# Seven half-depth products for eight in the gates and values of four chunks

## The chip, the core and the metric

The kernel runs on one core of a Trainium2 chip. It is one program, launched once; the metric is device microseconds of that core. Its engines are TensorE (PE in the profile, with PEld for its weight loads), VectorE (DVE), ScalarE (ACT) and GpSimd (POOL); SyncE (SP) issues most DMAs. Each engine takes its own instructions in the order of the program and waits at semaphores for the others.

## The reference

An attention with a learned position bias feeds a gated layer. What matters here is the second half:

```python
attn_out = _attn_ref(q, k, v, w1, b1, w2)                    # (4, 8, 576, 64)
x = attn_out.transpose(0, 2, 1, 3).reshape(2304, 512)
gate = 1.0 / (1.0 + np.exp(-(x @ w_gate)))                   # w_gate (512, 1536)
val = x @ w_val                                              # w_val  (512, 1536)
out = (gate * val) @ w_out                                   # w_out (1536, 512)
```

The weights come in as 64-bit floats, seen as pairs of 32-bit words; the kernel narrows them to 32 bits itself.

## The kernel before

The program has three stages: the position bias, the attention (32 units of one batch and two heads) and the gated layer, class `Moe`. The layer starts near 360 us, when the last unit of the attention leaves.

**Tiling.** The 2304 tokens are six chunks of `T = 384`; the 1536 hidden features are 12 blocks f of 128. For one pair of chunk c and block f, `gates` (L864) makes two products over a depth of 512 into the PSUM banks pg (gate) and pu (value). Every operand is split into a high part, which the matmul takes as it is, and a low part, the rest; a product is then high x high, high x low and low x high. So one product of 128 features by 384 tokens is 4 pieces of the depth x 3 = 12 matmuls of 384 columns, and a pair (c, f) has 24. `gated` (L875) forms g = sigmoid(pg) * pu on ACT and DVE and splits it into gh and gl. `outs` (L886) multiplies it by block f of w_out: 3 tiles of 128 tokens, 3 matmuls of 512 columns each, 9 in all, added up over f in the banks po. pg and pu have one bank each, po three banks for each of two chunks.

**Order.** The order on each engine is the order of the recording code (`run`, L904). The first 24 pairs follow the list ORDER (L46): chunk 0 (A) and chunk 1 (B) take turns, A leading, while the weights are made. After each pair `convert` (L848) moves the pipeline of weight blocks on: `stage` loads a raw block (512 KB), `narrow` makes 32-bit numbers of it with one ACT and four DVE instructions (L188 to L200), `upper` (L835) copies the high part on ACT and `lower` (L841) subtracts it on DVE. 30 of the 36 blocks (f and three kinds: gate z = 0, value z = 1, w_out z = 2) are made in this stretch; six were narrowed earlier and wait in DRAM (`scratch`). All split weights then stay in SBUF, in the pools wa, wb and wfirst.

The remaining 48 pairs are chunks 2 to 5, block by block. The next chunk's x is prepared meanwhile (`x_steps`, L946; for chunk 2 by XAFTER from the pair B5 on, the arithmetic from B9 on): two halves of the head sums are added, multiplied by the reciprocal softmax sum, and split.

What stands around the change on the queues: SP issues the loads of raw blocks, of x (xin) and reciprocals (xrec), and the stores, in the order of recording; POOL has no arithmetic in the layer after the attention's last pieces, since the sum of the head halves runs on DVE for all chunks but the first (XENG, L59).

## Time and profile before

| | us |
|---|---|
| median of 3 runs (lowest to highest) | 821.5 (821.01 to 823.13) |
| profiled execution | 824.66 |
| its span, first to last instruction | 822.5 |
| PE busy in the span | 794.6 (97%) |
| DVE busy | 506.2 (62%) |
| ACT busy | 431.0 (52%) |
| POOL busy | 260.8 (32%) |

The profile is of one execution. The span is what its rows cover; 2.2 us of the execution lie outside it. A matmul's row runs on while the next one streams, so rows overlap: the pace of PE is read from the starts of successive matmuls, or from the chain of waits, whose pieces do not overlap. A DVE row too can begin a little before the one ahead has ended.

### The profile page before, as it was taken

Reading aid. Unit: us, or ns where it says so; the run is one execution under the profiler, and the core shown is the slowest. Engines: PE = TensorE matmul, PEld = TensorE weight load, DVE = VectorE, ACT = ScalarE, POOL = GpSimd, SP = SyncE. Lnnn points to the kernel's source line nnn. Section 1 sums busy time; section 2 is a strip of 40 time slices with the busy share of each in tenths; the row PEclk is TensorE's granted clock in tenths of the full one; section 3 lists DMA queues with packets and bytes.
Section 4 is the critical chain, followed back from the end, with each engine's and each line's share of the span. In section 5 each row is a group of like instructions: output and inputs, shape, how many; then the busy total and the mean of one; then the engine's idle time right before and its main releaser. Section 6 shows DMA issues by size and latency. Waiting matters only on the chain.

```text
span 822.5 us, 16931 instructions
## 1 busy us (share of the span) xinstructions
PE 794.6 (97%) x6500; PEld 744.9 (91%) x6500; DVE 506.2 (62%) x1097; ACT 431.0 (52%) x914; POOL 260.8 (32%) x312
## 2 busy tenths in 40 slices
PE   7999989999999999879999999999999999999998
PEld 4888879999999998868999989999999999999997
DVE  6788789999899899977888784223311321241111
ACT  6888679898898998754444442211221221122112
POOL 1333569998999979730000000000000000000000
PEclk9999999999999999999999999999999999999999
DMA  5533236556466486569632302301030112011001
GB/s 193 170 104 116 67 87 169 148 149 181 142 171 178 122 229 189 175 188 314 228 94 63 100 2 77 97 21 29 10 116 1 40 48 68 4 35 39 1 1 38
DMA packets 51134, 86.40 MB, mean 105 GB/s; under 512 B 5616, under 2 KB 27248, under 8 KB 51056
## 3 DMA queue, kind: packets, MB, share of 16 engines
q1 hardware_dynamic: 48752, 81.87, 33.8%
q10 hardware_dynamic: 2304, 3.47, 1.3%
q8 instruction: 51, 0.84, 0.4%
q14 instruction: 27, 0.22, 0.1%
HBM read 60.08 MB, written 15.80 MB: 92 GB/s over the span
## 4 chain that ended last, share of the span: by engine, by line
PE 80%; DVE 10%; ACT 5%; issue 2%; DMA 2%; POOL 0%; POOLq 0%; SPq 0%; DVEq 0%; ACTq 0%
PE pu L872 18%; PE pg L872 17%; PE po L893 17%; PE sc L550 8%; PE acc L635 7%; PE pt L573 6%; PE bps L343 3%; PE y L319 2%; ACT ind L324 2%; DVE btmp L351 2%; DVE en L554 1%; PE pt L593 1%; DVE bias L359 1%; ACT en L557 1%; DVE aL L473 1%
## 5 line engine op out<-in xcount | busy, mean ns | idle before, releaser
L881 DVE TENSOR_TENSOR g<-pu,g 128x384 f32<-128x384 f32 x72 | 40.1, 557 | 204.3 <-PE pu L872 197.2
L872 PE MATMUL pg<-xhi,w 128*128 128x384 f32 x576 | 160.4, 339 | 3.7 <-ACT g L880 2.7
L872 PE MATMUL pu<-xhi,w 128*128 128x384 f32 x576 | 159.2, 336 | 0.4 <-DVE w L844 0.4
L893 PE MATMUL po<-w,gh 128*128 128x512 f32 x432 | 133.8, 391 | 0.0
L557 ACT ACTIVATE en<-en,mn 128x576 f32<-128x576 f32 x144 | 111.6, 775 | 31.4 <-DVE mn L554 30.4
L882 ACT ACTIVATE gh<-g 128x384 fp32r<-128x384 f32 x72 | 37.8, 525 | 145.3 <-DVE g L881 145.3
L550 PE MATMUL sc<-k,QS 128*128 128x288 f32 x640 | 111.5, 300 | 1.3 <-DVE bias L359 0.6
L872 PEld LDWEIGHTS pg<-xhi,w 128*128 128x128 f32 x576 | 105.6, 189 | 7.7 <-ACT g L880 3.1
L872 PEld LDWEIGHTS pu<-xhi,w 128*128 128x128 f32 x576 | 105.2, 188 | 1.0 <-DVE w L844 1.0
L554 DVE CUSTOM_DVE_ANT_0 en<-sc,bias 128x576 f32<-128x576 f32 x128 | 93.9, 752 | 7.4 <-PE sc L550 6.4
L872 PE MATMUL pg<-xlo,w 128*128 128x384 f32 x288 | 97.3, 338 | 0.2 <-DVE xlo L807 0.2
L872 PE MATMUL pu<-xlo,w 128*128 128x384 f32 x288 | 96.8, 336 | 0.0
L550 PEld LDWEIGHTS sc<-k,QS 128*128 128x128 f32 x640 | 91.7, 188 | 2.4 <-PE sc L550 0.8
L893 PEld LDWEIGHTS po<-w,gh 128*128 128x128 f32 x432 | 80.1, 188 | 12.0
L880 ACT ACTIVATE g<-pg 128x384 f32<-128x384 f32 x72 | 35.0, 487 | 106.1 <-PE pg L872 106.1
L573 PE MATMUL pt<-ident,en 128*128 128x128 f32 x576 | 87.1, 274 | 3.7 <-DVE aL L473 1.9
L893 PE MATMUL po<-w,gl 128*128 128x512 f32 x216 | 84.2, 390 | 0.0
L635 PE MATMUL acc<-aH,vv 128*128 128x288 f32 x240 | 75.7, 332 | 3.4 <-DVE xe L638 3.2
L573 PEld LDWEIGHTS pt<-ident,en 128*128 128x128 f32 x576 | 68.5, 141 | 7.2 <-ACT en L557 3.4
L473 DVE TENSOR_TENSOR aL<-pt,aH 128x512 fp32r<-128x512 f32 (+1 forms) x112 | 66.7, 607 | 7.2 <-ACT aH L472 7.2
L343 PE MATMUL bps<-cfs,ind 128*128 128x64 bf16 x1458 | 67.4, 193 | 3.0 <-DVE bias L359 2.2
L324 ACT ACTIVATE ind<-y 128x576 bf16<-128x576 f32 x100 | 62.4, 658 | 11.1 <-PE y L319 8.9
(121 smaller groups left out, 1425.9 us busy)
## 6 DMA issues: line engine op xcount, KB each, us to landing
kr<-in_k_dram SPq DMA_DIRECT2D x32, 288.0 KB
QS<-part SPq DMA_DIRECT2D x64, 144.0 KB, 2.7
xs<-xe SPq DMA_DIRECT2D x32, 288.0 KB, 3.4
xin<-xs SPq DMA_DIRECT2D x48, 192.0 KB, 3.4
vr<-in_v_dram SPq DMA_DIRECT2D x16, 320.0 KB, 3.4
qr<-in_q_dram SPq DMA_DIRECT2D x16, 288.0 KB
xrec<-rs SPq DMA_DIRECT2D x48, 96.0 KB, 3.6
ww<-in_moe_w_val_dram SPq DMA_DIRECT2D x9, 512.0 KB, 7.1
```

Source lines behind the costliest of these rows:

```text
L324: nc.scalar.activation(out=o, in_=y[:, :, 0:HF], func=AF.Sigmoid, scale=float(2.0 ** 64))
L343: nc.tensor.matmul(out=o, lhsT=st, rhs=cfs[:, part], start=(part == 0), stop=(part == 2))
L473: return lambda: nc.vector.tensor_tensor(out=lo, in0=ps, in1=hi.bitcast(F32), op=ALU.subtract)
L550: nc.tensor.matmul(out=ps[:, e, 0:HF], lhsT=l, rhs=r[:, HF * e:HF * e + HF], start=(i == 0), stop=(i == len(mms) - 1))
L554: nc.vector.tensor_tensor_reduce(out=half(en), in0=ps[:, :, 0:HF], in1=half(nbias), scale=-0.125, scalar=3.0e38, op0=ALU.add, op1=ALU.min, ...
L557: nc.scalar.activation(out=en, in_=en, func=AF.Exp, bias=mn, scale=-1.0, accum_out=sm)
L573: nc.tensor.transpose(pt[:, J], en[:, 128 * J:128 * J + 128], ident)
L635: nc.tensor.matmul(out=acc[:, 0:HF], lhsT=l, rhs=r, start=(i == 0), stop=(i == len(mms) - 1))
L872: self.nc.tensor.matmul(out=(pg, pu)[z], lhsT=l, rhs=r, start=(kc == 0 and i == 0), stop=(kc == 3 and i == 2))
L881: nc.vector.tensor_tensor(out=g, in0=pu, in1=g, op=ALU.mult)
L882: nc.scalar.activation(out=gh, in_=g, func=AF.Copy)
L893: self.nc.tensor.matmul(out=po, lhsT=l[:, tt], rhs=r, start=(f == 0 and i == 0), stop=(f == self.NF - 1 and i == 2))
```

## The change

Chunks 0 and 1 are computed as before. Chunks 2 and 3 (q = 1), then 4 and 5 (q = 2), are taken as a pair, blocks f = 2k and 2k + 1 as a pair, and the depth of 512 as two halves of 256. Gate (z = 0) and value (z = 1) of such a group are then a 2 x 2 by 2 x 2 product of blocks, made by the scheme with seven products and fifteen sums in place of eight products. One `half` (q, k, z) is seven products of 2 x 3 = 6 matmuls of 384 columns; there are 24 halves.

- Sums of x (`x_sums`): the four blocks B11 to B22 of a chunk pair and T1 to T4. POOL adds the head halves and makes the differences, DVE scales, ACT and DVE split the seven that are used. For q = 1 this is recorded between the pairs A and B, nine items after each from the 15th on; for q = 2 one item after each product, from the third half on.
- Sums of weights (`w_sums`): for each half the narrowed blocks are read again from DRAM, POOL makes four sums of 128 x 256, ACT and DVE split four tiles. This runs one to three halves ahead.
- So every narrowed gate and value block is now also written to `scratch`, and every split w_out block to `parts` (`keep`), from where it is read again for each chunk pair (`load_wo`).
- Sums of the products (`evict`): ACT copies the first product out of its bank, DVE does seven additions of a bank and an SBUF tile for each half. The banks pg and pu take turns, so product j + 2 needs the bank of product j.
- The output products of one group (12 tiles of 3 matmuls) stand one behind each product of the next group's first twelve products.
- SBUF pools: split weights share 13 slots of wa, raw blocks 15 of wb, which are given up for the x sums in the 15th pair; gates and their temporaries share 18 tiles.

```diff
+PRODUCTS = (("A11", "B11"), ("A12", "B21"), ("S2", "T2"), ("S3", "T3"), ("S1", "T1"), ("A22", "T4"), ("S4", "B22"))
@@ begin
+        def keep():
+            if z == 2:
+                nc.sync.dma_start(out=self.parts[f], in_=self.wts[b][2].bitcast(F32))
+            elif b not in self.pre:
+                nc.sync.dma_start(out=self.scratch[b], in_=m)
-        self.going[n] = steps + [(3, upper), (4, lower)]
+        self.going[n] = steps + [(3, upper), (4, lower), (6 if z == 2 else 4, keep)]
@@ x_sums
+            def add(n, t=t):
+                nc.gpsimd.tensor_tensor(out=t[n], in0=i[:, 0], in1=i[:, 1], op=ALU.add)
+            def scale(n, t=t):
+                nc.vector.tensor_tensor(out=t[n], in0=t[n], in1=t.pop((n, "rec")), op=ALU.mult)
+            def less(n, a, b, t=t):
+                nc.gpsimd.tensor_tensor(out=t[n], in0=t[a], in1=t[b], op=ALU.subtract)
+            def high(n, t=t, kc=kc):
+                nc.scalar.activation(out=var[n][:, 0, kc], in_=t[n], func=AF.Copy)
+            def low(n, t=t, kc=kc):
+                nc.vector.tensor_tensor(out=var[n][:, 1, kc], in0=t[n], in1=var[n][:, 0, kc].bitcast(F32), op=ALU.subtract)
+            for w in ("lB11 lB12 +B11 *B11 lB22 +B12 hB11 *B12 lB21 +B22 -B11 T1=B12-B11 *B22 +B21 hT1 T2=B22-T1 *B21 -T1 "
+                      "T3=B22-B12 hT2 hB22 T4=B21-T2 -T2 -B22 hT3 hB21 -T3 -B21 hT4 -T4").split():
@@ w_sums
+            for o, a, b, op in ((t[1][:, 0:2], m[:, 1, 0:2], m[:, 1, 2:4], ALU.add), (t[1][:, 2:4], t[1][:, 0:2], m[:, 0, 0:2], ALU.subtract),
+                                (t[2][:, 0:2], m[:, 0, 0:2], m[:, 1, 0:2], ALU.subtract), (t[2][:, 2:4], m[:, 0, 2:4], t[1][:, 2:4], ALU.subtract)):
+                nc.gpsimd.tensor_tensor(out=o, in0=a, in1=b, op=op)
@@ half
+            for kc in range(2):
+                for l, r in ((0, 0), (0, 1), (1, 0)):
+                    nc.tensor.matmul(out=p, lhsT=W[i][:, l, at + kc], rhs=V[b][:, r, kc], start=(n == 0), stop=(n == 5))
+        def add(o, p, x):
+            nc.vector.tensor_tensor(out=o, in0=p, in1=x, op=ALU.add)
+        for j in range(7):
+            p = product(j)
+            late, self.late = self.late, []
+            if self.now:
+                s = self.now.pop(0)()
...
+            evict(j, p)
+            for f in late:
+                f()
...
+            if nxt:
+                if j < 4:
+                    nxt[2][j]()
+                if 1 <= j < 5:
+                    nxt[3][j - 1]()
...
+            if self.fill:
+                self.fill.pop(0)()
@@ run
-        order += [(c, f) for c in range(2, NC) for f in range(NF)]
+            for h in range(len(self.halves)):
+                if h % NF == 2 and h < NF:
+                    self.fill = self.x_sums(2)
+                self.half(h)
```

On DVE, before, between the g of the pair A8 and the g of the next pair, B7 (g is the gated product, w a weight block, wm and ww its narrowed and raw form):

```order
881 L881 TENSOR_TENSOR g<-pu,g 128x384
882 L883 TENSOR_TENSOR gl<-g,gh 128x384
883 L844 TENSOR_TENSOR w_9_8317<-wm,w_9_8317 128x512
884 L194 TENSOR_SCALAR wm<-wm 128x512
885 L197 SCALAR_TENSOR_TENSOR wm<-ww,wm 128x512
886 L200 SCALAR_TENSOR_TENSOR wm<-ww,wm 128x512
887 L191 TENSOR_SCALAR wm<-wm 128x512
888 L881 TENSOR_TENSOR g<-pu,g 128x384
```

One weight block's worth of work stands between the two. The same place in the changed kernel (xt is a block of x or a difference T, xq its split form; L890 is the g):

```order
882 L890 TENSOR_TENSOR g<-pu,g 128x384
883 L892 TENSOR_TENSOR gl<-g,gh 128x384
884 L847 TENSOR_TENSOR w_9_8362<-wm,w_9_8362 128x512
885 L197 TENSOR_SCALAR wm<-wm 128x512
886 L200 SCALAR_TENSOR_TENSOR wm<-ww,wm 128x512
887 L203 SCALAR_TENSOR_TENSOR wm<-ww,wm 128x512
888 L194 TENSOR_SCALAR wm<-wm 128x512
889 L955 TENSOR_TENSOR xq<-xt,xq 128x384
890 L941 TENSOR_TENSOR xt<-xt,xrec 128x384 x2
891 L955 TENSOR_TENSOR xq<-xt,xq 128x384
892 L890 TENSOR_TENSOR g<-pu,g 128x384
```

Four instructions of the x sums now stand ahead of the second g; over the six pairs from B6 to A10 it is 19 of them, all ahead of the last value block of the weights.

On POOL, before, the end of its program:

```order
285 L466 TENSOR_SCALAR vv_7223<-vr 128x5x64
286 L477 TENSOR_TENSOR vv_7223<-vr,vv_7223 128x5x64
287 L761 MEMSET sig 128x1
288 L978 UNCONDITIONAL_BRANCH
289 L978 ISA
```

After the attention's last split POOL has nothing left. In the changed kernel the sums of x and then of the weights (ws, from a reloaded pair of blocks wm) follow there:

```order
287 L765 MEMSET sig 128x1
288 L938 TENSOR_TENSOR xt<-xin 128x384 x3
289 L945 TENSOR_TENSOR xt<-xt 128x384
290 L938 TENSOR_TENSOR xt<-xin 128x384
291 L945 TENSOR_TENSOR xt<-xt 128x384 x3
292 L938 TENSOR_TENSOR xt<-xin 128x384 x3
293 L945 TENSOR_TENSOR xt<-xt 128x384
294 L938 TENSOR_TENSOR xt<-xin 128x384
295 L945 TENSOR_TENSOR xt<-xt 128x384 x3
296 L984 TENSOR_TENSOR ws<-wm_8804 128x256
297 L984 TENSOR_TENSOR ws<-ws,wm_8804 128x256
```

Sixteen instructions of 128 x 384 stand before the first sum of weights, in the stretch where DVE makes the weights.

On DVE in a value half (z = 1) of the changed kernel (L1028 adds a bank pg or pu to a tile, L1038 multiplies value and gate, L1041 and L995 are low parts of gates and of weights):

```order
1138 L1028 TENSOR_TENSOR u_10293<-pu,u_10293 128x384
1139 L1041 TENSOR_TENSOR gl<-c_10197,gh 128x384
1140 L995 TENSOR_TENSOR wv<-ws,wv 128x512
1141 L1028 TENSOR_TENSOR u_10341<-pg,u_10293 128x384
1142 L995 TENSOR_TENSOR wv<-ws,wv 128x512
1143 L1028 TENSOR_TENSOR c_10362<-pu,u_10341 128x384
1144 L1028 TENSOR_TENSOR u_10293<-pu,u_10293 128x384
1145 L1038 TENSOR_TENSOR c_10251<-c_10362,c_10251 128x384
1146 L995 TENSOR_TENSOR wv<-wm_10149,wv 128x256
1147 L1028 TENSOR_TENSOR u_10341<-pg,u_10341 128x384
```

Where a pair (c, f) of the last chunks had a g and a gl on DVE, these rows are what stands behind three of a half's seven products.

## Rows read from the trace of the kernel before

**Rows 1.** The page: busy time of PE.
```profile
PE 794.6 (97%) x6500; PEld 744.9 (91%) x6500; DVE 506.2 (62%) x1097; ACT 431.0 (52%) x914; POOL 260.8 (32%) x312
```
**Rows 2.** Stages: busy us (count) by engine, granted clock, DMA share, GB/s.
```profile
360.00:521.60 161.60, 157.11 (x827) 146.37 (x826) 120.78 (x227) 66.44 (x122) 0.00 (x0) 0.99 0.40 128
521.60:820.00 298.40, 296.86 (x1573) 278.63 (x1571) 72.59 (x132) 62.22 (x122) 0.00 (x0) 1.00 0.12 37
```
**Rows 3.** The chain that ended last: start, us, what.
```profile
698.31 2.08 PE pg L872 x12
700.39 2.08 PE pu L872 x12
702.47 2.05 PE po L893 x9
```
**Rows 4.** Waits of PE from 355 us on: total us, times, longest.
```profile
PE pg L872 <- DVE w L844: 0.9, 1, 0.9
PE pu L872 <- DVE w L844: 0.4, 1, 0.4
```
**Rows 5.** DVE in order of time, pairs B6 to A11: start, us, [idle before].
```profile
458.13 0.56 DVE L881 TENSOR_TENSOR g<-pu,g 128x384 f32<-128x384 f32 x1 [0.91 <-PE pu L872]
459.28 0.56 DVE L883 TENSOR_TENSOR gl<-g,gh 128x384 fp32r<-128x384 f32 x1 [0.59 <-ACT gh L882]
...
465.21 0.55 DVE L881 TENSOR_TENSOR g<-pu,g 128x384 f32<-128x384 f32 x1
...
470.56 0.56 DVE L881 TENSOR_TENSOR g<-pu,g 128x384 f32<-128x384 f32 x1 [0.91 <-PE pu L872]
...
494.07 1.47 DVE L844 TENSOR_TENSOR w<-wm,w 128x512 fp32r<-128x512 f32 x2
```
**Rows 6.** Lines from 355 us on: count | busy us, mean ns | idle before.
```profile
L883 DVE TENSOR_TENSOR gl<-g,gh 128x384 fp32r<-128x384 f32 x72 | 40.2, 558 | 42.6 <-ACT gh L882 42.6
L882 ACT ACTIVATE gh<-g 128x384 fp32r<-128x384 f32 x72 | 37.8, 525 | 145.3 <-DVE g L881 145.3
L880 ACT ACTIVATE g<-pg 128x384 f32<-128x384 f32 x72 | 35.0, 487 | 106.1 <-PE pg L872 106.1
L844 DVE TENSOR_TENSOR w<-wm,w 128x512 fp32r<-128x512 f32 x30 | 20.5, 685 | 0.1
L839 ACT ACTIVATE w<-wm 128x512 fp32r<-128x512 f32 x30 | 18.7, 622 | 12.6 <-DVE wm L200 12.6
```
**Rows 7.** DVE in order of time while POOL works, two inputs in SBUF.
```profile
307.93 1.39 DVE L805 TENSOR_TENSOR xin<-xin,xrec 128x384 f32<-128x384 f32 x1
...
329.44 1.75 DVE L844 TENSOR_TENSOR w<-ww,w 128x512 fp32r<-128x512 f32 x1
...
350.17 1.59 DVE L807 TENSOR_TENSOR xlo<-xin,xhi 128x384 fp32r<-128x384 f32 x1
...
357.08 1.26 DVE L805 TENSOR_TENSOR xin<-xin,xrec 128x384 f32<-128x384 f32 x1
```
**Rows 8.** POOL in order of time in the same stretch.
```profile
307.62 1.28 POOL L477 TENSOR_TENSOR aL<-ar,aH 128x512 fp32r<-128x512 f32 x1
...
314.74 1.01 POOL L804 TENSOR_TENSOR xin<-xin 128x384 f32<-128x384 f32 x1
...
320.38 0.88 POOL L477 TENSOR_TENSOR vv<-vr,vv 128x320 fp32r<-128x320 f32 x1
...
350.06 1.29 POOL L477 TENSOR_TENSOR aL<-ar,aH 128x512 fp32r<-128x512 f32 x1
```
**Rows 9.** Lines of DVE from 150 to 300 us, where POOL is busy.
```profile
L473 DVE TENSOR_TENSOR aL<-pt,aH 128x512 fp32r<-128x512 f32 x50 | 34.2, 684 | 4.4 <-ACT aH L472 4.4
```
**Rows 10.** PE in order of time, after a wait: start, us, [idle before].
```profile
370.21 0.44 PE L872 MATMUL pg<-xhi,w 128*128 128x384 f32 x1 [2.69 <-ACT g L880]
```
**Rows 11.** The stage behind that wait: as rows 2.
```profile
372.00:374.00 2.00, 2.00 (x8) 2.00 (x7) 1.85 (x4) 0.94 (x2) 0.00 (x0) 0.50 0.93 218
```
**Rows 12.** DMA issues: count, KB each, us from issue to landing.
```profile
xin<-xs SPq DMA_DIRECT2D x48, 192.0 KB, 3.4
xrec<-rs SPq DMA_DIRECT2D x48, 96.0 KB, 3.6
ww<-in_moe_w_val_dram SPq DMA_DIRECT2D x9, 512.0 KB, 7.1
```

More of the change, by code (lines that the diff above doesn't have):

```diff
@@ L142, in tile_kernel @@
     scratch = dram.tile([3 * DFF // 128, 128, 4, 128], F32, name="scratch")
-    moe = Moe(tc, w_gate, w_val, w_out, scratch, xs, rs, out)
+    parts = dram.tile([DFF // 128, 128, 2, 4, 128], F32, name="parts")
+    moe = Moe(tc, w_gate, w_val, w_out, scratch, parts, xs, rs, out)
     with ExitStack() as right, ExitStack() as att:
@@ L828, in begin @@
         w = self.raw.pop(0)
-        if b in self.scratch:
+        if b in self.pre:
             m, steps = w, []
@@ L860, in convert @@
                 del self.going[n]
-        if news is not None:
+        if self.staged < len(self.blocks) and (self.staged < RAWS + SLOTS[1] or self.staged - self.begun < AHEAD):
             self.stage()
@@ L895, in store, with outs, tile_ @@
-    def store(self, c):
-        for t, po in enumerate(self.po.pop(c)):
-            if c == self.NC - 1 and t == 2:
-                ob = self.pools["xin"].tile([128, 2, self.T], F32, name="xin").rearrange("p s t -> p (s t)")[:, 0:DM]
-            else:
-                ob = self.pools["ob"].tile([128, DM], F32, name="ob")
-            self.nc.scalar.activation(out=ob, in_=po, func=AF.Copy)
-            self.nc.sync.dma_start(out=self.out[self.T * c + 128 * t:self.T * c + 128 * t + 128, :], in_=ob)
+    def outs(self, c, gh, gl, wo, last):
+        def tile_(t):
+            first = (c, t) not in self.po
+            if first:
+                self.po[c, t] = self.pools["ps_o"].tile([128, DM], F32, name=f"po{t}")
+            po, tt = self.po[c, t], slice(128 * t, 128 * t + 128)
+            oh, ol = (wo[:, i].rearrange("p k f -> p (k f)") for i in range(2))
+            for i, (l, r) in enumerate(((gh, oh), (gh, ol), (gl, oh))):
+                self.nc.tensor.matmul(out=po, lhsT=l[:, tt], rhs=r, start=(first and i == 0), stop=(last and i == 2))
+            return (lambda: self.store(c, t)) if last else None
+        return [lambda t=t: tile_(t) for t in range(self.T // 128)]
@@ L904, in run, with load_wo @@
+    def load_wo(self, f):
+        self.wos[f] = w = self.pools["wfirst"].tile([128, 2, 4, 128], F32R, tag="w", name="wo")
+        self.nc.sync.dma_start(out=w.bitcast(F32), in_=self.parts[f])
     def run(self):
@@ new lines, in run @@
+            self.e, self.late, self.now, self.next = {}, [], [], []
+            self.halves = [self.w_sums(k, z) for _ in range(NC // 2 - 1) for k in range(NF // 2) for z in range(2)]
+            todo = self.x_sums(1)
+            first = [self.halves[i][0] for i in (0, 1, 2)]
+            first += [self.halves[i][1] for i in (0, 1)]
+            first += [g for p in zip(*self.halves[0][2:]) for g in p]
+            self.do(START[0], nc.scalar)
+            before, opened = [], False
+            for i, (c, f) in enumerate(order):
+                while not {(f, 0), (f, 1)} <= self.full:
+                    self.convert()
+                ps = self.gates(f, *self.x[c], first=(i == 0))
+                stored = []
+                if before:
+                    while (before[0], 2) not in self.full:
+                        self.convert()
+                    stored = [o() for o in before[1](self.wts[before[0], 2][2])]
+                for _ in range(CONV[c] - 1):
@@ L934, in run @@
                     if self.going:
                         self.convert()
-                before = (c, f, *self.gated(*ps))
+                g = self.gated(*ps)
+                before = f, lambda w, c=c, g=g, last=(f == NF - 1): self.outs(c, *g, w, last)
                 if i == 0:
                     self.do(START[1], nc.scalar)
-                if stored is not None:
-                    self.store(stored)
-                if self.going:
+                for s in stored:
+                    if s:
+                        s()
@@ L942, in run @@
+                if self.going or self.raw or self.staged < len(self.blocks):
                     self.convert()
-                if 0 < c < NC - 1:
-                    self.x_steps(c + 1, x, xin, xrec, (XNEXT if c > 1 else XAFTER).get(f, ()))
-    def x_steps(self, c, x, xin, xrec, what, eng=None):
-        for w, kc in what:
-            if w == "l":
-                xin[kc] = self.load_x(c, kc, eng)
-            elif w == "r":
-                xrec[kc] = self.load_r(c, kc, eng)
-            else:
-                if kc == 0:
-                    x[c] = self.x_tiles(c)
-                for g in self.prep_x(c, xin.pop(kc), xrec.pop(kc), *x[c], kc):
-                    g()
+                if not opened and i >= XOPEN and self.begun > RAWS + SLOTS[1] and min(self.going, default=99) >= RAWS + SLOTS[1]:
+                    raws.close()
+                    self.open(ph, "left", xv=XVARS)
+                    opened = True
@@ new lines, in run @@
+                if opened:
+                    for _ in range(XRATE):
+                        if todo:
+                            todo.pop(0)()
+                    if i >= len(order) - 3:
+                        for _ in range(5):
+                            if first:
+                                first.pop(0)()
+            while self.going:
+                self.convert()
+            for g in todo + first:
+                g()
+            self.next = before[1](self.wts[NF - 1, 2][2])
```

196 lines of the change are left out of this document (148 added, 48 removed).

## The prediction

> **What bounds the kernel now.** I read the busy times of the page first: PE is busy for 794.6 of 822.5 us [rows 1], so the question is what keeps it from streaming, or how much it streams. The table by stage splits the layer in two. In the second, 521.6 to 820 us, PE leaves 1.5 us idle in 298.4, and DVE has 72.6 us of work [rows 2]. The chain of waits names there nothing but PE itself: 2.08 us for a gate product, 2.08 for a value product, 2.05 for the output product [rows 3], 6.21 us for a pair, and 48 pairs make 298.1. So this stage costs what its matmuls cost. In the first, up to 521.6 us, DVE is the close second: 120.8 us of 161.6 on average [rows 2], but while weights are made it does little else. Two of PE's waits there are already for a low part of weights that DVE makes, 0.9 and 0.4 us [rows 4]. DVE in order of time shows how much room is left: per two pairs, the g's at 458.13 and 470.56 are 12.43 us apart, which is twice a pair's 6.21, and of these DVE waits only 0.91 us for the product and 2 x 0.59 for ACT's gh in the middle of a turn [rows 5]. The last low parts, of the value and output blocks of f = 11, end at 495.5 (494.07 with 1.47) [rows 5].
>
> Two sums follow: what PE no longer streams, and what DVE now does in a place where it has no time.
>
> **The change part by part. (a) Products removed.** 48 pairs have 24 gate and value matmuls each, 1152; 24 halves have 7 x 6 = 42, 1008. So 144 go, at 2.083 / 12 = 0.1736 us each [rows 3]: **-25.0 us**. The output products stay (144 tiles of 3 matmuls, 2.05 / 3 = 0.684 us a tile). A group of two halves is then 14 x 1.04 + 12 x 0.684 = 22.8 us against four pairs' 24.9.
>
> **(b) x sums in the turns of DVE.** From B6 to A10 the order puts 19 x-sum instructions on DVE ahead of the last value block's low part: 8 scalings and 11 low parts of 128 x 384. The nearest rows are those of the same shape, two inputs in SBUF: 0.558 us [rows 6], with successive rows overlapping, so that the pace is 0.48 to 0.56; I take 0.50. 19 x 0.50 = 9.5 us; the turns give back two waits of 0.91 [rows 5], 1.8 in all. The half-waits of 0.59 for gh recur in every turn and can't be filled, since gl is next in program order. What is late on DVE is late on PE one for one, since PE waits for these weights before [rows 4]: **+7.7 us** (ends: 0, if the blocks have more lead than [rows 4] suggest; 19 x 0.56 = 10.6 with no wait filled).
>
> **(c) POOL beside DVE.** Before, POOL does nothing from 360 us on [rows 2]; now 15 of its 16 instructions for the x sums run before that last value block. While POOL works, rows of DVE with both inputs in SBUF become long: the scaling L805 takes 1.39 and 1.26 us where its shape takes 0.558 alone, the low part of weights 1.75 against 0.685, the low part of x 1.59 [rows 6, 7], each beginning while a POOL instruction of 0.88 to 1.29 us runs [rows 8]. Over the 11 such rows between 307.93 and 357.08 us the excess is 5.3 us, 0.48 a row. An instruction of DVE that reads one bank and one SBUF tile keeps its time beside a busy POOL: 0.684 us over 50 [rows 9]. Nearly all of what DVE does in the turns is of the first kind. One such row per POOL instruction: 15 x 0.48 = **+7.2 us** (ends: 0, if these instructions meet rows that aren't held; 15 x 1.01 = 15.2, POOL's length for this shape [rows 8], if each stops DVE throughout). The Trainium skill ("SBUF — State Buffer", section "Who interferes with whom") states that a DVE instruction with two SBUF inputs contends with a GpSimd instruction that reads SBUF, that one with a single SBUF input doesn't, and that the loser of the port is blocked and not slowed. The trace agrees on who is held (1.39 for 0.558; 0.684 unchanged); a block of full length would make the term 15.2 and the whole change slower, a rival below.
>
> A wait of PE has a second price: after the 2.69 us before 370.21 [rows 10] the granted clock falls to 0.50 from 372 to 374, that is to 1.2 GHz [rows 11]. Waits under 1 us leave the stage's mean at 0.99 [rows 2]. I expect the lateness of (b) and (c) in pieces of about 1 us at each pair, so nothing for it in the sum; one such stretch costs about 1.8 us and goes to the slower rival. The Trainium skill ("TensorE: Matmul & The Clock Gate", Part 1) states that an idle array drops to half rate, which rows 10 and 11 show here; by it, any single long wait would be paid twice.
>
> **(d) The first two halves.** The group before them is missing, so from the fourth product on no output tile stands behind a product. The value half h = 1 gives PE only 7 x 1.04 = 7.3 us. DVE has there 7 additions, 4 multiplications g and 4 gl at 0.48 to 0.56 [rows 6] (7.2 to 8.4) and the low parts of weights, 3 x 0.685 and one of half the width, 2.4: together 9.6 to 10.8, so 2.9 us too much in the mean. The gate half before it leaves 1.0 (7.3 for PE against 7 x 0.56 + 2.4 = 6.3). I take 1.9, and one low part of weights (0.7) for the passage from the pairs: **+2.6 us** (0 to 5).
>
> **(e) The other eleven value halves.** PE has 7 x 1.04 + 5 x 0.684 = 10.7 us, DVE 9.6 to 10.8, 10.2 in the mean: half a microsecond of slack, since product j + 2 needs the bank that DVE's addition for product j empties. The gate halves are roomy (12.1 against 6.3). POOL's four sums of weights in each half are 128 x 256; by the line through 1.28 us for 512 and 0.88 for 320 [rows 8] that is an estimate of 0.75 us each, so a hold of 0.36 by the proportion of (c). About two meet a held row: 0.7, less the slack 0.5, 0.2 us for each of seven halves. In four, x sums of the second chunk pair come on top, about one DVE row (0.4 beyond): 0.6. 7 x 0.2 + 4 x 0.6 = **+3.8 us** (ends: 0, if the gate halves' slack carries over; 11 x 1.0 = 11, two sums held for their full length).
>
> **At nothing.** DMAs: 18 narrowed blocks of 256 KB and 12 split w_out blocks of 512 KB are written, and about 1 MB is read again per half, 90 GB/s where the second stage moves 37 at a share of 0.12 [rows 2]; that share would grow to about 0.3. The loads go out one to three halves (8 us or more) ahead of their use, and such loads land in 3.4 to 7.1 us [rows 12]. On SP a store that waits for its block holds back the raw loads behind it, but those feed blocks used some 30 us later. If that cover fails, each late load costs what it is late, 1 to 3 us once at the start of the halves, which range (d) holds. ACT copies one bank and makes high parts, about 5 us of a half's 11 at 0.49 to 0.62 each [rows 6].
>
> **Sum.** -25.0 + 7.7 + 7.2 + 2.6 + 3.8 = **-3.7 us**. The rows are of an execution of 824.66 us, 822.5 of span and 2.2 outside it, 3.2 above the median of 821.5; a difference carries over, so **817.8 us**.
>
> **The rivals.**
> *Slower: POOL stops DVE for its whole instruction.* Place: the turns from B6 to A11, then the value halves. Price: 15.2 for 7.2 in (c), 11 for 3.8 in (e), and a clock stretch of 1.8: the sum becomes -25.0 + 7.7 + 15.2 + 2.6 + 11 + 1.8 = +13.3, 834.8 us. It decides from a mean hold of 0.6 us on: 15 holds and 22 of three quarters of the length make 31.5 units, and 3.7 / 31.5 = 0.12 above 0.48. At 0.75 with the clock it is 828. For it: rows with 1.0 us of excess (1.75 for 0.685, 1.59 for 0.558) [rows 7]; against: the mean excess of 0.48. I set 830 as its middle.
> *Little hold.* POOL's 15 instructions mostly meet the 1-input rows or DVE's own waits for gh, and the halves run at PE's pace: -25.0 + 7.7 + 2.6 = -14.7, 806.8 us. For it: DVE's 0.59 waits recur in each turn [rows 5], and a held row can eat one. Against: the rest of the 12.43 us, all but 2.1, is work.
> *Nearly all hidden.* The x sums too go beside PE: -25.0 to -21.5, 796.5 to 800 us. Against it stand PE's own waits for these weights [rows 4].
> *The change doesn't do what it says* can be left out: the order shows 42 matmuls for each half and no others.
>
> **How the numbers follow.** Forecast 0.42 with its own range of 812 to 824; slower rival 0.25 (826 to 835); little hold 0.25 (801 to 812); hidden 0.08. A measurement of this kernel can tell about 0.3% from no change: 2.5 us, 819.0 to 824.0. Of the forecast's 0.42, 0.25 lies below 819.0, 0.16 between, 0.01 above. Faster 0.25 + 0.25 + 0.08 = 0.58, same 0.16, slower 0.26. A range of 801 to 831 leaves out the hidden case and the upper half of the slower one, 0.2 in all.
>
> **What would show it.** (a): a group of two halves takes 22.8 us in the stages without x sums (4 to 10 of the 12 groups), on PE's chain. (b) and (c): PE's last pair A/B begins about 15 us later than before, with waits of about 1 us for low parts of weights in each pair from B6 on, and DVE's rows of two SBUF inputs at 1 us and more beside POOL. Wrong if those waits are under 5 us in sum (little hold) or over 20. (d): about 3 us of PE's waits in the first two halves. (e): value halves near 11 us; wrong if they take 12 or more, when DVE bounds them. Waits of PE for a DMA would refute the cost of nothing for the re-read weights.

## The result: slower by 1.3%

The changed kernel takes 832.3 us (median of 4 runs, 831.4 to 835.9); the kernel before, in the runs beside it, 822.3. The ratio is 1.0131 (95% interval 1.0097 to 1.0165). The forecast was 817.8; the rival "POOL stops DVE" had 830 as its middle. The profiled execution took 835.9 us.

The page's busy line, which answers to [rows 1]:

```profile
PE 785.9 (94%) x6356; PEld 726.9 (87%) x6356; DVE 669.4 (80%) x1357; ACT 492.3 (59%) x1046; POOL 380.8 (46%) x440
```

PE has 144 matmuls fewer, and still the span is longer, 834.1 for 822.5 us: PE's idle time went from 28 to 48 us, and DVE has 163 us more to do. The same view by stage as [rows 2] (busy us by engine, granted clock, DMA share, GB/s), cut at the first product of the halves and at half 11 (halves are numbered from 0):

```profile
460.00:538.60 78.60, 64.77 (x316) 58.35 (x315) 56.97 (x92) 28.67 (x57) 24.96 (x23) 0.93 0.50 158
538.60:671.30 132.70, 126.10 (x637) 113.07 (x636) 112.29 (x186) 55.39 (x116) 64.42 (x66) 1.00 0.43 135
671.30:829.80 158.50, 158.05 (x814) 145.24 (x812) 107.88 (x196) 61.53 (x124) 31.00 (x40) 1.00 0.26 87
```

Only the last stretch runs as forecast, with PE busy throughout. In the first PE idles 13.8 us and its clock is below full, in the second it idles 6.6 us. PE's waits in the layer, where [rows 4] had 0.9 and 0.4 us:

```profile
PE pg L880 <- ACT g L889: 8.8, 5, 3.4
PE pg L880 <- DVE w L847: 5.8, 2, 5.6
PE pu L1023 <- DVE u L1028: 3.1, 5, 1.0
PE pg L1023 <- DVE u L1028: 2.7, 4, 1.0
PE pu L880 <- DVE w L847: 2.6, 3, 1.2
```

Of the first row 3.4 us lie at the layer's start, like the 2.69 of [rows 10]; the other waits are new.

I split the layer at two marks that every trace has: the *stage* runs from the first gate product to the first half's first product, the *halves* from there to the end of the last output product (in the kernel before, the 48 pairs). Their lengths are read from the starts of these matmuls in PE's order of time; here the first and the second mark:

```profile
362.99 0.34 PE L880 MATMUL pg<-xhi,w 128*128 128x384 f32 x1
...
538.58 1.22 PE L1023 MATMUL pg<-xq,wv 128*128 128x384 f32 x6
```

Before: 157.1 and 301.1 us. After: 175.6 and 291.2. So the stage lost 18.5 us and the halves won 9.9. (What lies ahead of the layer ended at 357 to 363 us in the traces of this study, with the same code, so a single trace's total is read with care and these two lengths are compared.)

### The profile page after: what moved, and what is told of

The parts are those of the page before. It is cut to its first block, busy times and chain, and to the rows that moved or that the text cites. A ratio compares the mean times of both kernels' runs of the same rounds, so it can differ in the third digit from the quotient of the medians.

```text
span 834.1 us, 17462 instructions
## 1 busy us (share of the span) xinstructions
PE 785.9 (94%) x6356; PEld 726.9 (87%) x6356; DVE 669.4 (80%) x1357; ACT 492.3 (59%) x1046; POOL 380.8 (46%) x440
## 4 chain that ended last, share of the span: by engine, by line
PE 68%; DVE 18%; ACT 5%; issue 4%; DMA 3%; POOL 2%; SPq 0%; ACTq 0%; DVEq 0%; POOLq 0%
PE po L905 14%; PE pg L1023 9%; PE pu L1023 8%; PE sc L553 8%; PE acc L638 7%; PE pt L576 6%; PE pu L880 4%; PE pg L880 4%; PE bps L346 3%; PE y L322 2%; ACT ind L327 2%; DVE btmp L354 2%; DVE u L1028 1%; PE pt L596 1%; DVE xq L955 1%
## 5 line engine op out<-in xcount | busy, mean ns | idle before, releaser
L1023 PE MATMUL pg<-xq,wv 128*128 128x384 f32 x504 | 103.4, 340 | 3.3 <-DVE u L1028 2.7
L1023 PE MATMUL pu<-xq,wv 128*128 128x384 f32 x504 | 102.9, 339 | 3.7 <-DVE u L1028 3.1
L1023 PEld LDWEIGHTS pg<-xq,wv 128*128 128x128 f32 x504 | 89.3, 188 | 13.4 <-ACT gh L1040 3.4
L1023 PEld LDWEIGHTS pu<-xq,wv 128*128 128x128 f32 x504 | 89.5, 188 | 12.3 <-DVE u L1028 5.7
L905 PE MATMUL po<-wo,gh 128*128 128x512 f32 x288 | 89.6, 392 | 0.0
L880 PE MATMUL pg<-xhi,w 128*128 128x384 f32 x192 | 57.0, 357 | 14.6 <-ACT g L889 8.8
L346 PE MATMUL bps<-cfs,ind 128*128 128x64 bf16 x1458 | 67.4, 193 | 3.1 <-DVE bias L362 2.2
L327 ACT ACTIVATE ind<-y 128x576 bf16<-128x576 f32 x100 | 62.4, 657 | 11.1 <-PE y L322 8.9
L638 PE MATMUL acc<-aL,vv 128*128 128x288 f32 x240 | 67.7, 298 | 0.0
L346 PEld LDWEIGHTS <-ind 128*128 128x128 bf16 x1458 | 58.6, 98 | 9.8 <-DVE bias L362 4.1
L480 POOL TENSOR_TENSOR aL<-ar,aH 128x512 fp32r<-128x512 f32 x48 | 62.2, 1295 | 4.0
L475 ACT ACTIVATE aH<-pt 128x512 fp32r<-128x512 f32 (+1 forms) x112 | 57.4, 528 | 2.2 <-PE pt L576 2.2
```

What stands on the lines that cost most here:

```text
L327: nc.scalar.activation(out=o, in_=y[:, :, 0:HF], func=AF.Sigmoid, scale=float(2.0 ** 64))
L346: nc.tensor.matmul(out=o, lhsT=st, rhs=cfs[:, part], start=(part == 0), stop=(part == 2))
L480: nc.gpsimd.tensor_tensor(out=lo, in0=src, in1=hi.bitcast(F32), op=ALU.subtract)
L638: nc.tensor.matmul(out=acc[:, 0:HF], lhsT=l, rhs=r, start=(i == 0), stop=(i == len(mms) - 1))
L880: self.nc.tensor.matmul(out=(pg, pu)[z], lhsT=l, rhs=r, start=(kc == 0 and i == 0), stop=(kc == 3 and i == 2))
L905: self.nc.tensor.matmul(out=po, lhsT=l[:, tt], rhs=r, start=(first and i == 0), stop=(last and i == 2))
```

## The experiments

All are edits of the changed kernel. Ratios are to the kernel before, with the 95% interval; lengths in us. "From 16" is the last part of the stage, from the first gate product of the 16th pair, the first one with x sums ahead of it, to the end of the stage.

| run | ratio | interval | stage | from 16 | halves |
|---|---|---|---|---|---|
| before | 1 |  | 157.1 | 57.4 | 301.1 |
| changed | 1.0131 | 1.0097 to 1.0165 | 175.6 | 75.3 | 291.2 |
| e1 no x sums, first pair of chunks | 0.9872 | 0.9802 to 0.9942 | 156.6 | 57.5 | 291.6 |
| e2 no x sums, second pair | 1.0040 | 1.0011 to 1.0070 | 175.2 | 76.0 | 285.4 |
| e3 no stores of blocks | 1.0153 | 1.0093 to 1.0213 | 179.7 | 78.4 | 292.4 |
| e4 POOL's x sums on DVE | 1.0078 | 1.0045 to 1.0111 | 172.3 | 73.5 | 292.0 |
| e13 POOL's part alone | 1.0029 | 1.0001 to 1.0057 | 167.7 | 67.9 | 291.8 |
| e14 DVE's part alone | 1.0029 | 0.9998 to 1.0059 | 169.5 | 70.3 | 291.3 |
| e15 no weight sums | 1.0025 | 1.0003 to 1.0048 | 176.7 | 77.5 | 283.5 |
| e5 other pace | 1.0167 | 1.0128 to 1.0207 | 174.2 | 75.3 | 293.7 |
| e6 second x sums in gate halves | 1.0090 | 1.0059 to 1.0122 | 175.0 | 76.0 | 289.3 |
| e7 gl later | 1.0080 | 1.0048 to 1.0112 | 173.4 | 74.5 | 291.2 |
| e8 e5 + e6 + e7 | 1.0077 | 1.0046 to 1.0107 | 169.8 | 71.1 | 291.5 |
| e9 e8, order of the tail | 1.0022 | 0.9991 to 1.0053 | 169.9 | 69.6 | 290.2 |
| e10 e9, second x sums on DVE | 1.0001 | 0.9972 to 1.0030 | 169.4 | 70.5 | 290.7 |
| e11 e9, stores behind | 1.0039 | 1.0015 to 1.0063 | 170.8 | 71.9 | 291.4 |
| e12 e11 + DVE as e10 | 1.0023 | 0.9995 to 1.0050 | 171.5 | 72.7 | 288.6 |
| e16 e12, queues | 0.9992 | 0.9967 to 1.0016 | 166.5 | 67.9 | 288.8 |
| e17 e16, stores spread | 0.9981 | 0.9962 to 1.0000 | 165.8 | 67.4 | 290.7 |
| e18 e17, weight sums in gate halves | 0.9997 | 0.9973 to 1.0022 | 166.1 | 67.3 | 291.1 |

Each length is read from one trace, and traces differ where the code is the same. The first four pairs are alike in the changed kernel and in e1, e2, e4 to e6 and e13 to e15, and take 30.4 to 31.9 us there: a difference of the stage of up to 1.5 us can stem from its start alone. "From 16" is free of that; the changed kernel, e2 and e6 are alike in it and have 75.3 to 76.0. The halves are alike in the changed kernel and in e1, e4, e7, e13 and e14, and have 291.2 to 292.0. So a difference of less than a microsecond between two traces shows nothing.

### What made the stage late

**e1, e2: x sums replaced by loads.**
```diff
-                if "=" in w:
+                if q in LOADED:                             # e1: (1,), e2: (2,)
+                    items.append((lambda n=w[1:], kc=kc: fetch(n, kc)) if w[0] == "h" else lambda: None)
+                elif "=" in w:
...
```


> Leaves out the arithmetic of the x sums of chunks 2 and 3: the 14 split tiles are loaded from DRAM instead (their values are then not the sums). Everything else stands. Theory D (DVE has no room for these instructions in the turns, and POOL's share of them holds DVE): the stretch from the first gate product to the first half, 175.6 us in the changed kernel and 157.1 before, goes back to 157 to 159, the whole to about 815. Rival K (the stores of narrowed blocks keep their tiles, ACT waits for one, and the sigmoid behind it is late): the stretch stays at 163 to 166, with PE's waits for ACT's g of 4 us, the whole at 820 to 823.

> Leaves out the arithmetic of the x sums of chunks 4 and 5 in the same way (tiles loaded from DRAM). Theory D: the halves 2 to 11, which take 12.0 us and more on average beyond what halves 12 to 23 take, fall to the pace of those (12.2 and 10.9 us), which is 9 to 11 us, and the whole comes to 821 to 823. Rival S (the additions that empty the banks and the sums of weights bound the first halves by themselves): less than 3 us, 829 to 832.

e1's stage is back at 156.6, and its part from the 16th pair at 57.5 where the kernel before has 57.4: all that the change costs there is in these sums. The kernel is then faster than the one before, 0.9872. e2 takes 5.8 us off the halves, less than the 9 to 11 expected: halves 2 to 11, where these sums stood, take 117.5 us and not 124.3, 6.8 less, and half 1, which the edit leaves alone, takes 1.1 more. Theory D holds for the stage, and in the halves something else takes a part.

**e3: no stores of blocks.** In the changed kernel's chain of waits one piece is such a store, ahead of ACT's part of the next block and the sigmoid behind that:
```profile
472.23 6.31 DMA scratch<-wm
...
478.65 0.67 ACT wm L191
```
```diff
-        self.going[n] = steps + [(3, upper), (4, lower), (6 if z == 2 else 4, keep)]
+        self.going[n] = steps + [(3, upper), (4, lower)]
...
```


> Leaves out the stores of narrowed and split blocks; the halves re-read the blocks that were narrowed early, as many bytes as before (their values are then those of other blocks). Rival K: PE's waits for ACT's g of 2.0 us at 480 and 504 us go, and with them the slow clock behind: 5 to 7 us less, 825 to 827. Theory D: DVE is as late as before, the waits move to the low parts of weights: less than 2 us, 830 to 833.

The stage did not become shorter (179.7, and from the 16th pair 78.4 for 75.3), and the whole is not below the changed kernel: the waits moved to other places. Rival K falls. A piece on the chain need not be worth its length: DVE was as late beside it.

**e13, e14: the two halves of the same work.**
```diff
-                nc.vector.tensor_tensor(out=t[n], in0=t[n], in1=t.pop((n, "rec")), op=ALU.mult)
+                r = t.pop((n, "rec"))
+                if q == 2:                                  # e13: for q = 1 no scaling; low parts are loaded
...
+                if q == 1:                                  # e14: no differences, and no adding of head halves
+                    t[n] = t[a]
+                    return
...
```


> Of the x sums of chunks 2 and 3 only POOL's 16 instructions and ACT's high parts are left; DVE's scalings and low parts are left out (the low tiles are loaded from DRAM, no reciprocals are loaded). Theory D+H (DVE's own work and POOL's hold both count): the stretch up to the first half, 156.6 us without any of these sums and 175.6 with all, comes to 162 to 167 by a hold of 0.5 to 0.7 us an instruction. If POOL's hold is nothing beside an unfilled DVE: 157 to 159.

> The other half: of the x sums of chunks 2 and 3 DVE's 22 instructions and ACT's are left, POOL's 16 are left out (a head half stands for the sum, a block for the difference). Theory D+H: 163 to 167 us for the stretch, by 19 x 0.5 less 1.8 us and the slow clock behind the waits; with e13 the two parts then make up the 19 us. If POOL and its chain were the whole cause: 157 to 159.

From the 16th pair on, e13 takes 10.4 us more than e1 and e14 12.8 more. Put on top of the other, DVE's part adds 7.4 us (from e13 to the changed kernel) and POOL's 5.0 (from e14). So both count, each at or a little above what was expected. That the two differences from e1 make 23.2 us and all the sums together only 17.8 has a reason in the edits: both runs keep ACT's 14 high parts, about 0.5 us each, which e1 leaves out, so what they cost is counted twice. No run leaves them out by themselves. DVE in order of time in e13, where it has none of the new instructions:

```profile
495.55 1.52 DVE L847 TENSOR_TENSOR w<-wm,w 128x512 fp32r<-128x512 f32 x1
496.99 1.21 DVE L197 TENSOR_SCALAR wm<-wm 128x512 int32<-128x512 int32 x1
498.23 1.37 DVE L200 SCALAR_TENSOR_TENSOR wm<-ww,wm 128x512 int32<-128x512 int32 x1
499.64 1.37 DVE L203 SCALAR_TENSOR_TENSOR wm<-ww,wm 128x512 int32<-128x512 int32 x1
500.93 1.21 DVE L194 TENSOR_SCALAR wm<-wm 128x512 f32<-128x512 f32 x1
502.07 0.54 DVE L890 TENSOR_TENSOR g<-pu,g 128x384 f32<-128x384 f32 x1
```
and POOL beside it:
```profile
495.25 1.27 POOL L938 TENSOR_TENSOR xt<-xin 128x384 f32<-128x384 f32 x1 [0.51 <-DMA xin<-xs]
496.48 1.44 POOL L947 TENSOR_TENSOR xt<-xt 128x384 f32<-128x384 f32 x1
497.88 1.18 POOL L938 TENSOR_TENSOR xt<-xin 128x384 f32<-128x384 f32 x1
499.02 3.98 POOL L947 TENSOR_TENSOR xt<-xt 128x384 f32<-128x384 f32 x3
```

Six POOL instructions in a row, and five DVE rows in a row are 0.7 to 0.8 us longer than alone (L847 takes 0.68 at 503.68). The sixth, with one input in PSUM, is not, though POOL still runs. Between 464 and 516.5 us 16 DVE rows of e13 have 11.4 us of such excess for 16 POOL instructions, 0.71 each; the changed kernel has 8.7 us in 12 rows, 0.73 a held row, for as many POOL instructions, 0.54 each. L197 and L194 read one SBUF tile and no bank, and are held like the rows with two inputs in SBUF (1.21 us; alone, at 504.28, L197 takes 0.42). In e4 and e14, where POOL rests, no row there has any.

**e4: POOL's 16 instructions on DVE.**
```diff
-                nc.gpsimd.tensor_tensor(out=t[n], in0=i[:, 0], in1=i[:, 1], op=ALU.add)
+                (nc.vector if q == 1 else nc.gpsimd).tensor_tensor(out=t[n], in0=i[:, 0], in1=i[:, 1], op=ALU.add)
...
```


> Moves POOL's 16 instructions of the x sums of chunks 2 and 3 (adding the head halves, differences) to DVE. DVE's rows beside POOL show 8.7 us of excess in that stretch; 16 instructions at a pace of 0.5 are 8.0. Theory D: the stretch changes by less than 2 us, the whole stays at 830 to 833. Rival H (POOL's chain and its hand-overs to DVE, ACT and back are what is late, not DVE's work): 4 us or more less, 828 and below. Rival P (POOL's hold was small): 5 us or more longer, 837 and above.

The stage is 3.3 us shorter, of which 1.8 lie behind the start of the 16th pair (73.5 for 75.3, or for the 76.0 of e2 and e6). So theory D's "less than 2" is about met: leaving these instructions on POOL cost DVE at least as much as doing them itself. The held rows say the same, 8.7 us against 16 x 0.5 = 8.0. That DVE is the better place by a little is likely, and near the limit of what two traces can tell.

**The slow clock.** PE's longest wait in the changed kernel:
```profile
510.94 1.01 PE L880 MATMUL pg<-xhi,w 128*128 128x384 f32 x2 [5.59 <-DVE w L847]
```
The stretch of this wait and the one behind it, as in [rows 11]:
```profile
504.00:510.00 6.00, 0.61 (x2) 0.30 (x2) 5.34 (x7) 1.51 (x4) 3.06 (x3) 0.83 0.49 189
510.00:514.00 4.00, 3.06 (x10) 3.06 (x11) 3.93 (x8) 1.67 (x4) 0.69 (x1) 0.50 0.00 0
```
In steps of 2 us from 440 to 544, busy time times the missing share of the clock makes 3.4 us, against 13.8 idle; in the kernel before 0 against 1.1, in e1 0 against 2.7. The Trainium skill ("TensorE: Matmul & The Clock Gate", Part 1) says that an idle array goes to half rate; these rows show it, 0.50 being 1.2 GHz.

### What made the halves late

**e15: no weight sums on POOL.**
```diff
+            t[0], t[1], t[2], t[3] = m[:, 0], m[:, 1], m[:, 0], m[:, 1, 2:4]
+            return
```


> The 96 sums of weights on POOL are left out (the blocks themselves are split and used in their place). If POOL's hold in the halves is what makes halves 1 to 11 long: the stretch of the halves falls from 291.2 by 5 us or more. If DVE's own instructions (additions, low parts, x sums) fill these halves: by 1 to 3 us.

The halves are 7.7 us shorter, 5.9 of it in halves 2 to 11. These halves in the changed kernel and in e15:
```profile
558.18:682.47 124.29, 119.20 (x601) 107.15 (x601) 103.66 (x173) 49.80 (x104) 58.96 (x60) 1.00 0.37 116
552.82:671.20 118.38, 117.78 (x600) 107.54 (x601) 95.96 (x173) 49.85 (x104) 18.00 (x16) 1.00 0.39 123
```
DVE is busy 7.7 us less with the same 173 instructions, so it is POOL's hold, and not DVE's own work alone. (e15 also takes POOL out of the chain that leads to ACT's and DVE's parts of the weights, but PE's waits in these halves are for DVE's additions and not for weights.) DVE by line in the changed kernel from half 0 to half 11 (count | busy us, mean ns | idle before):

```profile
L1028 DVE TENSOR_TENSOR u<-pg,u 128x384 f32<-128x384 f32 x28 | 15.3, 548 | 4.1 <-PE pg L1023 4.0
L955 DVE TENSOR_TENSOR xq<-xt,xq 128x384 fp32r<-128x384 f32 x14 | 10.2, 731 | 0.0
L1041 DVE TENSOR_TENSOR gl<-u,gh 128x384 fp32r<-128x384 f32 x10 | 8.5, 875 | 0.1
L995 DVE TENSOR_TENSOR wv<-ws,wv 128x512 fp32r<-128x512 f32 x23 | 20.3, 884 | 0.0
```

The additions that read a bank keep 0.55 us; rows of the same shape with both inputs in SBUF average 0.73 and 0.88, and the low parts of weights 0.88 where [rows 6] have 0.685. The Trainium skill ("SBUF — State Buffer", section "Who interferes with whom") draws the line at the second SBUF input for DVE instructions outside the two-port modes, a limit that the prediction left out, and these rows agree. The Trainium skill counts tensor_scalar there among the instructions that can use these modes, and L197 above was held with one input. The Trainium skill says there too that of the two the one that comes second is blocked fully. A held row of the stage lost about 0.7 us beside POOL instructions of about 1.2; such an average does not decide it, since a row that comes late in a POOL instruction would have only the rest of it to wait for.

**e6: second x sums in gate halves alone.**
```diff
-            if self.fill:
-                self.fill.pop(0)()
+            for _ in range(2 if z == 0 else 0):
+                if self.fill:
+                    self.fill.pop(0)()
```


> The x sums of chunks 4 and 5 are recorded two items after each product of a gate half and none in a value half, in place of one after each product of both. Theory D: DVE has 5.8 us of room in a gate half and none in a value half, so the halves 2 to 10 lose 4 to 5 us of their excess; the stretch of the halves falls from 291.2 to 286 to 288, the whole to 827 to 829. Rival S (the excess is POOL's hold on DVE wherever it falls): less than 1.5 us.

The halves are 1.9 us shorter, between the two: a gate half has some room. That POOL's hold goes there with the sums, and so eats the rest, is argued and not shown.

### Does a better place exist?

**e5, e7, e8: pace, gl behind the next low part, and both with e6.**
```diff
+        items[17:17] = [items.pop(30), items.pop(30)]       # e5, e8: two loads ahead
-                    for _ in range(XRATE):
+                    for _ in range(3 if i < 20 else 12):
...
-        nc.vector.tensor_tensor(out=gl, in0=g, in1=gh.bitcast(F32), op=ALU.subtract)
+        self.late.append(lambda: nc.vector.tensor_tensor(out=gl, in0=g, in1=gh.bitcast(F32), op=ALU.subtract))
...
```


> The x sums of chunks 2 and 3 are only recorded at another pace: 3 items after each pair up to the 20th and 12 after each later one, in place of 9 after each, with two loads moved ahead. Ahead of the last value block's low part stand then 5 of their DVE instructions in place of 19; the others come where DVE makes no weights any more. Theory D (DVE is late by what stands ahead of the last weights): the stretch up to the first half falls from 175.6 us to 160 to 164, the whole to 817 to 822. Rival C (the chain load, POOL, DVE, ACT of the x sums is too long to fit behind the weights): the first half waits instead, the stretch stays above 168.

> In the 24 pairs the low part gl of the gates is recorded behind the next low part of weights and no longer right behind ACT's gh, so that DVE does not wait 0.59 us for gh in each pair. Nothing else changes. Theory D: DVE gains 0.6 us in each of the seven pairs in which it is late, 4 us, and the stretch falls from 175.6 to 170 to 172 us, the whole to 827 to 829. Rival L (the lateness is set by other things than DVE's time, POOL's results or loads): less than 1.5 us.

> The three edits together: pace of the first x sums, the second x sums in gate halves alone, gl behind the next low part of weights. Theory D: the stretch up to the first half 158 to 160 us, the halves 286 to 288, the whole 811 to 816, below the kernel before. If the first half waits for its x sums (rival C) the stretch is above 164 and the whole above 817.

e7's stage is 2.2 us shorter, but only 0.8 of it lies behind the start of the 16th pair, where the edit was to win 4: that is rival L's range, and hardly more than the spread. In e8 the same edit goes with fewer sums, and from the 16th pair on e8 takes 4.2 us less than e5. There all pairs from the fifth to the twentieth take 6.2 to 6.3 us, so with fewer sums and the 0.59 us back the weights come in time so far (the 21st takes 10.1 us, in the kernel before 7.7); but then the first half waits 11.1 us for what was put off (10.6 in e5). Rival C won that place: a chain load, POOL, DVE, ACT, DVE behind the weights.

**e9 to e12, e16 to e18: the order of that tail.**
```diff
+                    for _ in range(3 if i == 20 else 0):      # e9: weight loads ahead of the last x items
+                        first.pop(0)()
+                    for _ in range(3 if i < 20 else 14):      # ... 14 items a pair, sums of weights behind
+                (nc.vector if q == 2 else nc.gpsimd).tensor_tensor(out=t[n], in0=i[:, 0], in1=i[:, 1], op=ALU.add)  # e10, e12
...
+                for s in stored:                              # e11: moved behind the x items; 4 and 12 items a pair
+                    if s:
+                        s()
+                t[n, "in"], t[n, "rec"] = self.load_x(c, k), self.load_r(c, k, r=self.etile("rec") if q == 1 else None)  # e16
+        (self.nc.sync if c else self.nc.scalar).dma_start(out=self.out[self.T * c + 128 * t:self.T * c + 128 * t + 128, :], in_=ob)  # e16
+                pending += [s for s in stored if s]       # e17: one store behind each pair
+            if z == 0 and j in (3, 6) and h + j // 3 + 1 < len(self.halves):  # e18: weight sums of two halves in a gate half
...
```


> As e8, but behind the weights the order is mended: the loads for the sums of weights of the first halves go out before the last x loads, their sums on POOL stand behind the x sums (in e8 eight of them stood ahead of the last four and waited 3.9 us for their loads), and the x items come 14 to a pair. Theory D with rival C for the tail: the first half's 11 us wait falls to 0 to 4, the stretch up to the first half to 159 to 163 us, the first half to 10 to 11, the halves in sum 287 to 289, the whole 812 to 817. If the wait stays above 8 us, not the order on POOL but the loads or the chain's own length set it.

> As e9_tail, and POOL's 16 instructions of the x sums of chunks 4 and 5 go to DVE, in the gate halves. By POOL's hold (about 0.7 us of DVE for each of its instructions, 0.5 on DVE itself) halves 2 to 10 become 2 to 3 us shorter than in e9_tail; if DVE's own work is what counts (little hold), they become 4 us or more longer.

> As e9_tail, with the three output stores of chunk 0 recorded behind the x items of their pair (in e9 they stood ahead of two x loads on SP and of ACT's parts of the x sums, and the third waited 2.5 us for its buffer), the first halves' weight loads behind the x loads, and 4 items a pair before the weights' end, 12 after it. If the loads and stores made the tail of e9 late, its two pairs of 11.0 us go back to 6.2 to 8, the stretch up to the first half from 169.9 to 160 to 164, and the whole to 813 to 818, below the kernel before. If the chain POOL, DVE, ACT is itself too long for the place, the stretch stays above 167.

> As e11, with the x sums of chunks 4 and 5 on DVE in place of POOL (as e10 against e9, where halves 2 to 10 were 1.0 us shorter in sum): within 2 us of e11.

> As e12 with 3 items a pair before the weights' end and 14 after it; the reciprocals of chunks 2 and 3 have tiles of their own, so that SP doesn't wait for one that DVE still has to free, three x blocks are loaded ahead, and the output stores of chunk 0 go out on ACT's queue. If the late loads on SP made the tail of e11 and e12 late (two pairs of 10 to 11 us), these pairs fall to 6.2 to 8, the stretch to 161 to 165, the whole to 812 to 818. If the chain itself is too long for the place: above 167 again.

> As e16, with the three output stores of chunk 0 one behind each of the last pairs. In e16 the third store's copy on ACT waited 3.7 us for its buffer with the next sigmoid behind it, and PE waited 4.65 us for that, at the slow clock afterwards. If that is what is left in the tail, the pair of 11.0 us falls to 6.2 to 7.5 and the next of 9.6 to 7 to 9, the stretch to 160 to 163, the whole to 815 to 819, below the kernel before. If not, PE waits there for another part of the chain and the stretch stays above 164.

> As e17, with the weight sums of two halves recorded in each gate half and none in a value half. POOL's instructions then meet DVE where it has room: the value halves fall from 11.1 to 10.8 and the early ones by 0.5 more, 2 to 5 us in sum, the whole to 811 to 816. If the sums now come too late for the value halves' low parts, these become longer instead.

Each moved the wait and none removed it. e10's x sums on DVE made halves 2 to 10 of e9 1.0 us shorter, not 2 to 3, and half 1 took 1.1 longer; e12 is within 2 us of e11. e9 cut the first half's wait to 3.2 us, and two pairs before it grew to 11.0 each; e11 and e12 changed little; e16, with the loads free of DVE, made the stage 166.5. Its third store's copy then held a sigmoid for 4.65 us; in e17 that pair takes 6.2 and the last pair 13.6:

```profile
PE pg L1030 <- ACT wv L997: 7.3, 1, 7.3
PE pg L1030 <- DVE wv L1002: 0.4, 1, 0.4
```

e17's stage is 0.7 us shorter, within the spread. So the store was not the bound. The chain waited for a load there; SP's issues and POOL behind them in e17:

```profile
506.02 5.62 SPq L984 DMA_DIRECT2D wm<-scratch  x6
511.74 1.25 SPq L791 DMA_DIRECT2D xin<-xs  x2
518.38 1.04 POOL L944 TENSOR_TENSOR xt<-xin 128x384 f32<-128x384 f32 x1 [5.98 <-DMA xin<-xs]
```

The last x load stands behind six loads for the weight sums; POOL is idle for 6.0 us until it has landed, and DVE for 3.3 behind it. So the tail is not bound by the arithmetic of the chain alone, and no run has this load ahead of the others. e18 brought nothing more. e16 to e18 stand level with the kernel before; e17's interval touches 1. No run beat both kernels clearly with all sums in it.

## Why the prediction was wrong

The sum had 3.7 us less; the medians are 10.0 us apart the other way. By the two lengths, 3.6 us of the miss lie in the stage (18.5 for 14.9) and 8.7 in the halves (9.9 won for 18.6).

- **(a) 25.0 us for 144 matmuls**: right. Halves 12 to 22 take 12.2 and 10.8 to 11.1 us where the sum had 12.1 and 10.7.
- **(b) and (c), 14.9 us for the stage**: right in mechanism, 3.0 short (17.9 us from the 16th pair on; 18.5 by the marks). On top of each other DVE's part measured 7.4 us and POOL's 5.0, against 7.7 and 7.2. What was left out: the slow clock (3.4), taken at nothing because the lateness was to come in pieces of 1 us at each pair. It came in a few long waits, 5.59 us the longest. In (c) a held row lost 0.73 us and not 0.48, but 12 rows were held and not 15, 8.7 us in all. 0.48 was too low for a held row because three of the 11 rows behind it were not held, in the kernel before:

```profile
312.21 0.54 DVE L807 TENSOR_TENSOR xlo<-xin,xhi 128x384 fp32r<-128x384 f32 x1
313.04 0.59 DVE L807 TENSOR_TENSOR xlo<-xin,xhi 128x384 fp32r<-128x384 f32 x1
325.84 0.55 DVE L805 TENSOR_TENSOR xin<-xin,xrec 128x384 f32<-128x384 f32 x1
```

  The other eight have 0.66 each. That nearly all of DVE's rows in the turns have two inputs in SBUF was misread: two of the five of a weight block have one, and they are held as well (L197 in e13).
- **(d) 2.6 us for the first two halves**: right in size. They take 9.83 and 9.77; with three output tiles in the first, 9.34 and 7.29 were PE's own: 3.0. (Half 1 takes 9.8 to 10.9 us in the runs that have the same code there.)
- **(e) 3.8 us for the other halves: the step that failed.** Halves 2 to 11 take 124.3 us where PE's own work is 114.0, 10.3 too many, and the rest another 2.4: 12.7 us for 3.8. Of the 10.3, 6.1 us lie in the five gate halves, which the prediction called roomy (12.1 us of PE against 6.3 of DVE) and priced at nothing. Half 4 takes 14.1 us, and DVE is busy for 13.7 of them:

```profile
583.18:597.29 14.11, 13.08 (x63) 11.23 (x64) 13.71 (x20) 5.56 (x12) 11.22 (x11) 1.00 0.05 19
```

  Its 20 DVE rows are not the 7 additions and 4 low parts of weights alone: six are left over from the value half before (an addition, two multiplications, three low parts of gates), three are of the x sums, and POOL holds most of those that read no bank. The term that was mis-sized most is the x sums of the second pair: 1.6 us, one DVE row in each of four value halves; there are 60 items, one to a product, so nearly nine halves of both kinds have them, and without them halves 2 to 11 are 6.8 us shorter (e2). The hold by the weight sums had about the right size on DVE (two rows of 0.36 a half are 7.2 us in ten halves; 7.7 measured, e15), but the slack taken off it and the room in the gate halves were not there: without the weight sums these ten halves are 5.9 us shorter, and all of them 7.7.
- **DMAs at nothing**: no wait of PE is for a DMA, and leaving the stores out won nothing (e3).
- **The slower rival** had the place and the sign, and came near the time, 832.3 for its 830; that it came so near is luck. Its mechanism, POOL stopping DVE for its whole instruction, had 15.2 us in (c), where the held rows make 8.7; it was to decide from a mean hold of 0.6 us on, 9.0 for its 15 instructions there, so by its own measure it was at the border. What made up for it is (e), 12.7 us for its 11, and the slow clock, 3.4 for its 1.8.

What stays open: how the 17.8 us of the x sums in the stage divide among DVE, POOL and ACT. The slow clock is in e13 and e14 too (1.7 and 3.4 us by the same count), so 1.7 of the 5.4 us by which their two differences exceed the whole are counted twice there; ACT's high parts have no run of their own. And whether POOL holds more rows here than before because it works in runs, with fewer pauses beside which a DVE row may fall, is only argued.

## What to carry to other kernels

Work that is moved to an idle engine is not free when that engine holds a full one: count for each of its instructions what the other loses, from rows where both run, and look at whether they run in a row. Before fewer matmuls are paid for with more vector work, find the stretch in which the vector engine sets the pace, and check that none of the new work falls there; here the x sums cost 18 us in such a stretch, more than the 9.9 us that the halves won. A step that seems to hide in "roomy" places is counted item by item over all the places that the program gives it, with what the half before leaves over.

## What the runs showed of the hardware

GpSimd's instructions lengthen too when DVE works beside them: 128 x 384 took 1.28 and 1.22 us on average in the changed kernel (1.01 in [rows 8]), and 128 x 256 took 0.85 to 0.89, where e8 has eight of 0.72 one after the other while DVE waits. Moving 16 GpSimd instructions of two SBUF inputs to a full DVE did not make the stage longer, but 1.8 us shorter from the 16th pair on (e4). A DVE tensor_scalar of 128 x 512 with one SBUF input was held as well, 1.21 us for 0.42 (e13). Which of the two is held can turn on which began first: in the kernel before, the DVE row at 325.84 above kept its time, and the POOL row that began 0.05 us later took 1.24 us for the 0.88 of [rows 8]:

```profile
325.89 1.24 POOL L477 TENSOR_TENSOR vv<-vr,vv 128x320 fp32r<-128x320 f32 x1
```

That is one instance.
